# One ScalarE pass for the first layer's activation, and seven half-block products for its group 3

## The chip, the cores and the metric

The kernel runs on one core of one Trainium2 chip. TensorE (PE) multiplies matrices into PSUM, VectorE (DVE) and ScalarE (ACT) read PSUM and SBUF, GpSimd (POOL) works on SBUF alone, and SyncE (SP) issues most of the transfers. The metric is device time in microseconds (us) of one launch. Before the change the median of three runs is 619.27 us (618.97 to 619.82).

## The reference

Three stages follow each other: a windowed attention, then two feed-forward layers over its output (1536 tokens of 512 values).

```python
# attention, 2 x 8 heads, 768 tokens, head_dim 64: near scores in a window, block scores against a max per 32 keys
scores = concat(where(mask, q @ k.T * scale, -1e9), q @ kmax.T * scale + log(32))
x = softmax(scores) @ concat(v, vmean)              # -> (1536, 512)
# layer one, w_in 512 x 2048, w_out 2048 x 512
h = x @ w_in
g = h * (1.0 / (1.0 + exp(-1.702 * h)))
x = g @ w_out
# layer two, w_gate and w_val 512 x 1536, w_out2 1536 x 512
out = (1 / (1 + exp(-(x @ w_gate))) * (x @ w_val)) @ w_out2
```

## The kernel before, in words

The layers' weights are split in groups of 256 hidden columns (two blocks of 128, called f = 0 and 1): eight groups in layer one, six in layer two. The tokens are three blocks of 512 (blk 0, 1, 2). Every float32 matrix is kept as a high part and a low part (`xH`, `xL`; `w..H`, `w..L`; `gh`, `gl`), and one product of 128x128 by 512 tokens is three matmuls (low by high, high by low, high by high).

**First half of a group.** `first` (L496) computes h of one token block by `project` (L477): 12 matmuls for each f. For layer one, ACT then takes a Sigmoid of 1.702 h out of PSUM into a tile `sg` (L501), DVE multiplies h by it (`gate_by`, L485), ACT rounds the result to `gh` (L493) and POOL writes the rest, `gl` (L494). With `batch=True`, used beside the attention, the matmuls of both f come first, then both sigmoids, then both multiplications. `second` (L523) multiplies `gh`, `gl` by the output weights: 24 matmuls a block into four PSUM tiles, each then added to `acc` by DVE (L557).

**Seven products instead of eight.** For groups from `PAIRED` on, `pair` (L381) computes blk 0 and 1 together. Seen as a 2 by 2 matrix product (two halves of the input dimension LO and HI, two token blocks, two f), it takes seven half-size products of 6 matmuls rather than eight. For that it needs sums of inputs, `input_sums` (L229: eight DVE operations of 1024 elements a partition, L234, four ACT casts, four POOL subtractions), sums of the group's weights (`load`, L148 to L167: four small DVE subtractions, one ACT cast, one DVE subtraction), and it takes copies of three partial results out of PSUM on ACT (L407, L431) and two additions on DVE (L410). blk 2 goes through `single` (L448). `input_sums` is a generator; `run` steps it once for each step of the main work, from the place where `folding` is set (L919); it stops before its last steps until group `PAIRED - 1` is done with block 1, since it overwrites `xH[1]`, `xL[1]`.

**What sets the order.** The code issues work in the order that its generators yield; a scheduler then orders each engine's instructions, so an edit can move others. Beside the attention a `filler` (L825) runs groups 0 and 1 for blk 0 and 1; after it come groups 2 and 3 and the pairs. The last steps of layer one make sums of its output (`token_sums`, L274) for layer two, which pairs in the same way.

Of the kernel before, what the change touches and what calls it, by code (L numbers as in the profile page):

```python
# [9 lines left out]
F32 = mybir.dt.float32  # L10
# [3 lines left out]
AF = mybir.ActivationFunctionType  # L14
# [3 lines left out]
P = 128  # L18
# [11 lines left out]
def attention_moe_moe2_kernel(ctx: ExitStack, tc: tile.TileContext, ins: dict, out: bass.AP):  # L30
    nc = tc.nc
# [17 lines left out]
    TB = 512  # L49
# [3 lines left out]
    scale = 1.0 / float(D) ** 0.5  # L53
# [33 lines left out]
    sg_slots, gh_slots, gl_slots = (Slots(t) for t in ("sg", "gh", "gl"))  # L87
# [108 lines left out]

    mats = {1: [w_in, w_out], 2: [w_gate, w_val, w_out2]}
    pieces, weights, raws = [], {}, []
    PAIRED = 4
    wanted = [(1, g, i) for g in range(n1) for i in range(2)] + [(2, 0, i) for i in range(3)]  # L200
    for g in range(1, n2):
        wanted += [(2, h, i) for h, i in ((g, 0), (g - 1, 2), (g, 1)) if (h, i) != (0, 2)]
# [178 lines left out]
    def pair(layer, g):  # L381

        def sums_of(n, i):
            return tuple(x[:, n] for x in weights[layer, g, i, "s"])

        def a(i, r, c):
            return tuple(block(x, r, c) for x in weights[layer, g, i])

        b11, b21, b22 = ((xH[n][:, h], xL[n][:, h]) for n, h in ((0, LO), (0, HI), (1, HI)))
        left = {
            "1": lambda i: a(i, 0, 0), "2": lambda i: a(i, 0, 1), "3": lambda i: sums_of(3, i),
            "4": lambda i: a(i, 1, 1), "5": lambda i: sums_of(0, i), "6": lambda i: sums_of(1, i),
            "7": lambda i: sums_of(2, i),
        }
        right = {"1": b11, "2": b21, "3": b22, "4": tsum["4"], "5": tsum["1"], "6": tsum["2"], "7": tsum["3"]}
        bank = {"1": "x", "2": "x", "5": "v", "3": "v", "6": "y", "7": "y", "4": "y"}
        ps, held, sg = {}, {}, {}

        def new(b, i):
            ps[b, i] = ps_f.tile([P, TB], F32, name=f"ps_{b}")
            return ps[b, i]

        def keep(n, i, p):
            held[n, i] = sg_slots.tile([P, TB], F32, "sg")
            nc.scalar.copy(held[n, i], p)  # L407

        def total(n, i, p):
            nc.vector.tensor_tensor(out=held[n, i], in0=p, in1=held[n, i], op=ALU.add)  # L410
            return held[n, i]

        def out(i, to, x, own=None):
            if layer == 1:
                gate = sg_slots.tile([P, TB], F32, "sg")
                nc.scalar.activation(gate, x, AF.Sigmoid, scale=1.702)
                gate_by((1, g, *to), x, gate)
                return
            if i:
                gate_by((2, g, *to), x, sg.pop(to))  # L420
                return
            sg[to] = own if own is not None else sg_slots.tile([P, TB], F32, "sg")
            nc.scalar.activation(sg[to], x, AF.Sigmoid)

        for n in ("1526374", "1256734")[layer - 1]:
            for i in range(layer):
                b = bank[n]
                p = new(b, i) if n in "15" else ps[b, i]
                product(p, left[n](i), right[n], n in "15")
                if n == "1":  # L430
                    nc.scalar.copy(new("y", i), p)  # L431
                elif n == "2":
                    out(i, (0, 0), p)
                elif n == "5":
                    keep("5", i, p)
                elif n == "6":
                    keep("6", i, p)
                elif n == "7":
                    t = total("5", i, p)
                    out(i, (1, 1), t, t)  # L440
                elif n == "3":
                    t = total("6", i, p)
                    out(i, (1, 0), t, t)
                else:
                    out(i, (0, 1), p)
                yield

    def single(layer, g):  # L448

        for f in range(GF):  # L450
            sg = None
            for i in range(layer):
                wh, wl = weights[layer, g, i]
                ps = ps_f.tile([P, TB], F32, name="ps_h" if i == 0 else "ps_v")
                for j in range(2):
                    half = (LO, HI)[j]
                    product(ps, (block(wh, f, j), block(wl, f, j)), (xH[2][:, half], xL[2][:, half]), j == 0)
                    if j == 0:
                        yield
                if i == 0:  # L460
                    sg = sg_slots.tile([P, TB], F32, "sg")
                    nc.scalar.activation(sg, ps, AF.Sigmoid, scale=1.702 if layer == 1 else 1.0)
                if i == layer - 1:
                    gate_by((layer, g, 2, f), ps, sg)
                yield

    acc, gt = {}, {}
# [15 lines left out]
    def gate_by(to, val, sg):  # L483

        nc.vector.tensor_tensor(out=sg, in0=val, in1=sg, op=ALU.mult)  # L485
        split(to, sg)

    def split(to, sg):
        name = "_".join(map(str, to))
        gh = gh_slots.tile([P, TB], F32R, f"gh{name}")  # L490
        gl = gl_slots.tile([P, TB], F32R, f"gl{name}")
        gt[to] = gh, gl
        nc.scalar.copy(gh, sg)  # L493
        nc.gpsimd.tensor_tensor(out=gl, in0=sg, in1=gh, op=ALU.subtract)  # L494

    def first(layer, g, blk, batch=False):  # L496
        w = weights[layer, g, 0]

        def sigmoid(layer, ps):
            sg = sg_slots.tile([P, TB], F32, "sg")  # L500
            nc.scalar.activation(sg, ps, AF.Sigmoid, scale=1.702 if layer == 1 else 1.0)  # L501
            return sg

        def gated(f, ps, sg):
            gate_by((layer, g, blk, f), ps, sg)

        if batch:
            held = []
            for f in range(GF):
                held.append(project(w[0], w[1], f, blk, "ps_h"))  # L510
                yield
            held = [(ps, sigmoid(layer, ps)) for ps in held]
            yield
            for f, (ps, sg) in enumerate(held):
                gated(f, ps, sg)
            yield
            return
        for f in range(GF):
            ps = project(w[0], w[1], f, blk, "ps_h")
            gated(f, ps, sigmoid(layer, ps))  # L520
            yield

    def second(layer, g, blk, last, lag=False):  # L523
# [355 lines left out]
    with tc.manual_schedule(engines={mybir.EngineType.SP}):  # L879
# [29 lines left out]
        for step in steps:  # L909
            need((*step[:2], 0))  # L910
            run(first(*step))
            if step[2] == 2:
                drop(*step[:2], 0)
            if prev:
                need((*prev[:2], 1))
                run(second(*prev, False))
                if prev[2] == 2:
                    drop(*prev[:2], 1)
            if step == (1, 2, 0):  # L919
                folding = itertools.islice(sums_1, 8)  # L920
            elif step == (1, PAIRED - 1, 1):
                for _ in folding:
                    pass
                folding = sums_1
            prev = step
# [101 lines left out]
```

## Time and profile before

| what | value |
|---|---|
| median of three runs | 619.27 us |
| the profiled execution's own time | 619.4 us |
| its span, first to last instruction | 617.6 us |
| mean granted TensorE clock | 0.997 |
| busy: PE, DVE, ACT, POOL | 603.2, 465.9, 307.3, 212.7 us |

The span is what the profile can be read on; 1.8 us lie around it. A busy share says how much of the span an engine was at work, not whether it was waited for. A matmul's own duration (0.39 us) is a latency, as matmuls overlap: the pace is the distance between two starts. What counts is where PE stood idle, and what it did between.

### The profile page before, as it was taken

What the parts mean: (1) busy time and instruction counts of PE and PEld (TensorE: products, weight loads), DVE (VectorE), ACT (ScalarE), POOL (GpSimd) and SP (SyncE); (2) the same over time, 40 slices, a digit from 0 to 9 for tenths busy, and PEclk for the clock granted to TensorE, in tenths of its full rate; (3) what the DMA queues carried; (4) which work ended last, traced back from release to release, by engine and by line L of the source; (5) the groups of instructions that cost most, each with busy time, mean ns of one, the idle gap of its engine ahead of it and who ended that gap; (6) DMA issues with size and microseconds to landing.
All of it is one profiled execution on the core that took longest, in us unless ns stands there. A gap on an engine that the chain in (4) does not pass through costs nothing.

```text
span 617.6 us, 8819 instructions
## 1 busy us (share of the span) xinstructions
PE 603.2 (98%) x3354; PEld 501.7 (81%) x3354; DVE 465.9 (75%) x684; ACT 307.3 (50%) x614; POOL 212.7 (34%) x168
## 2 busy tenths in 40 slices
PE   7798999999999999999999999999999999999997
PEld 4676777788878888888888898888898898898896
DVE  6699665389998778797769889577969768877434
ACT  4688657556443353435445566635335335444230
POOL 6797585323363423233231232022122021131030
PEclk9899999999999999999999999999999999999999
DMA  9998753034221104040102013321312222100014
GB/s 314 347 313 286 232 137 70 1 121 153 68 69 68 53 17 137 1 137 10 60 0 69 1 40 101 132 69 33 105 69 69 68 69 70 68 1 1 0 49 156
DMA packets 25161, 58.10 MB, mean 94 GB/s; under 512 B 1568, under 2 KB 1824, under 8 KB 25120
## 3 DMA queue, kind: packets, MB, share of 16 engines
q1 hardware_dynamic: 24400, 56.24, 28.0%
q10 hardware_dynamic: 720, 1.31, 0.6%
q8 instruction: 26, 0.43, 0.3%
q14 instruction: 15, 0.12, 0.1%
HBM read 53.08 MB, written 3.15 MB: 91 GB/s over the span
## 4 chain that ended last, share of the span: by engine, by line
PE 81%; DVE 8%; ACT 3%; issue 3%; DMA 2%; POOL 2%; SPq 0%; ACTq 0%; POOLq 0%; DVEq 0%
PE ps_o L474 32%; PE ps_y L178 15%; PE ps_x L178 10%; PE ps_v L178 10%; PE ps_h L474 5%; PE ps_h L178 4%; PE ps_s L692 2%; ACT e L705 1%; PE ps_x L744 1%; DMA raw<-in_moe_w_out 1%; POOL gl L494 1%; DMA vt<-in_vt 1%; PE ps_p L725 1%; DVE da L137 1%; DVE w_0L L142 1%
## 5 line engine op out<-in xcount | busy, mean ns | idle before, releaser
L494 POOL TENSOR_TENSOR gl<-sg,gh 128x512 fp32r<-128x512 f32 x84 | 125.9, 1505 | 362.1 <-ACT gh L493 256.2
L557 DVE TENSOR_TENSOR acc<-ps_o,acc 128x512 f32<-128x512 f32 x143 | 95.9, 683 | 46.7 <-PE ps_o L474 46.6
L474 PE MATMUL ps_o<-gl,w_1H 128*128 128x512 f32 x192 | 75.5, 394 | 0.5 <-POOL gl L494 0.5
L493 ACT CAST gh<-sg 128x512 fp32r<-128x512 f32 x84 | 51.5, 620 | 48.0 <-DVE sg L485 38.6
L474 PE MATMUL ps_o<-gh,w_1H 128*128 128x512 f32 x192 | 74.6, 390 | 0.0
L474 PE MATMUL ps_o<-gh,w_1L 128*128 128x512 f32 x192 | 72.1, 396 | 1.9 <-ACT gh L493 1.7
L474 PE MATMUL ps_o<-w_2L,gh 128*128 128x512 f32 (+1 forms) x146 | 56.6, 388 | 0.0
L474 PE MATMUL ps_o<-w_2H,gh 128*128 128x512 f32 (+1 forms) x146 | 56.2, 386 | 0.0
L474 PE MATMUL ps_o<-w_2H,gl 128*128 128x512 f32 (+1 forms) x146 | 56.2, 389 | 0.1
L137 DVE SCALAR_TENSOR_TENSOR da<-da,db 128x1024 uint32<-128x1024 uint32 x34 | 46.1, 1357 | 5.7 <-ACT da L131 5.1
L131 ACT ACTIVATE da<-da 128x1024 f32<-128x1024 f32 x34 | 36.1, 1061 | 24.7 <-DVE da L123 22.9
L474 PEld LDWEIGHTS ps_o<-gh,w_1L 128*128 128x128 f32 x192 | 35.9, 188 | 9.9 <-ACT gh L493 2.3
L474 PEld LDWEIGHTS ps_o<-gl,w_1H 128*128 128x128 f32 x192 | 36.0, 188 | 8.5 <-POOL gl L494 1.5
L474 PEld LDWEIGHTS ps_o<-gh,w_1H 128*128 128x128 f32 x192 | 36.1, 188 | 7.3
L705 ACT ACTIVATE e<-ps_s,nm 128x128 f32<-128x128 f32 x96 | 34.2, 377 | 9.6 <-DVE nm L697 7.1
L681 POOL TENSOR_SCALAR kx<-k 128x384 f32<-128x384 f32 x24 | 33.3, 1389 | 14.6 <-PE ps_s L692 7.5
L474 PE MATMUL ps_h<-xH,w_0L 128*128 128x512 f32 x96 | 37.7, 401 | 0.0
L474 PE MATMUL ps_h<-xL,w_0H 128*128 128x512 f32 x96 | 37.6, 392 | 0.0
L474 PE MATMUL ps_h<-xH,w_0H 128*128 128x512 f32 x96 | 37.5, 390 | 0.0
L485 DVE TENSOR_TENSOR sg<-ps_h,sg 128x512 f32<-128x512 f32 x32 | 21.7, 682 | 14.1 <-ACT sg L501 11.9
L474 PEld LDWEIGHTS ps_o<-w_2H,gh 128*128 128x128 f32 x146 | 27.4, 188 | 5.8
L474 PEld LDWEIGHTS ps_o<-w_2L,gh 128*128 128x128 f32 x146 | 27.5, 188 | 4.9
(242 smaller groups left out, 1504.5 us busy)
## 6 DMA issues: line engine op xcount, KB each, us to landing
raw<-in_moe_w_out SPq DMA_DIRECT2D x13, 1024.0 KB, 4.9
raw<-in_moe_w_in SPq DMA_DIRECT2D x8, 1024.0 KB, 7.0
raw<-in_moe_w_gate SPq DMA_DIRECT2D x6, 1024.0 KB, 5.1
raw<-in_moe_w_val SPq DMA_DIRECT2D x6, 1024.0 KB, 5.1
q<-in_q SPq DMA_DIRECT2D x20, 256.0 KB, 8.5
vwin<-in_v SPq DMA_DIRECT2D x6, 768.0 KB, 8.6
k<-in_k SPq DMA_DIRECT2D x8, 400.0 KB, 7.2
out<-acc SPq DMA_DIRECT2D x11, 256.0 KB, 2.0
```

The source lines that it names most:

```text
L131: nc.scalar.activation(af, af, AF.Prelu, scale=REBIAS, alpha=-2.0 ** 32)
L137: nc.vector.scalar_tensor_tensor(out=a, in0=a, scalar=3, in1=b, op0=ALU.logical_shift_left, op1=ALU.bitwise_or)
L142: nc.vector.tensor_tensor(out=lo.rearrange(flat), in0=af, in1=hi.rearrange(flat), op=ALU.subtract)
L178: nc.tensor.matmul(ps, lhsT=a[x][:, kk, :], rhs=b[y][:, kk, :], start=start and i == 0, stop=i == n - 1, skip_group_check=True,)
L474: nc.tensor.matmul(ps, lhsT=a, rhs=b, start=i == 0, stop=i == n - 1)
L485: nc.vector.tensor_tensor(out=sg, in0=val, in1=sg, op=ALU.mult)
L493: nc.scalar.copy(gh, sg)
L494: nc.gpsimd.tensor_tensor(out=gl, in0=sg, in1=gh, op=ALU.subtract)
L557: nc.vector.tensor_tensor(out=a[:, m, :], in0=ps, in1=a[:, m, :], op=ALU.add)
L681: nc.gpsimd.tensor_scalar(out=to, in0=x, scalar1=scale, scalar2=None, op0=ALU.mult)
L692: nc.tensor.matmul(ps[:, j, :], lhsT=t[:, j, :], rhs=kt[:, j, :], start=False, stop=j == G - 1)
L705: nc.scalar.activation(e[:, j, :], s[:, j, :], AF.Exp, bias=nm[:, j:j + 1], accum_out=sm[:, j:j + 1])
```

## The change

Layer one's gate is written by one ACT pass of `Gelu_apprx_sigmoid` from PSUM (or from the summed tile) into `sg`, through a new helper `gated`; Sigmoid and DVE's multiplication go. Layer two keeps its Sigmoid and multiplication. `PAIRED` goes from 4 to 3, so group 3 is computed by `pair` and `single`, and `load` makes weight sums for it. `folding` starts at step (1, 1, 2) rather than (1, 2, 0); the operations in `input_sums` stay on the engines that they were on.

```diff
-    PAIRED = 4
+    PAIRED = 3
...
         def out(i, to, x, own=None):
             if layer == 1:
-                gate = sg_slots.tile([P, TB], F32, "sg")
-                nc.scalar.activation(gate, x, AF.Sigmoid, scale=1.702)
-                gate_by((1, g, *to), x, gate)
+                gated((1, g, *to), x)
                 return
...
-                if i == 0:
-                    sg = sg_slots.tile([P, TB], F32, "sg")
-                    nc.scalar.activation(sg, ps, AF.Sigmoid, scale=1.702 if layer == 1 else 1.0)
-                if i == layer - 1:
-                    gate_by((layer, g, 2, f), ps, sg)
+                gated((layer, g, 2, f), ps)
                 yield
...
+    def gated(to, x):
+
+        sg = sg_slots.tile([P, TB], F32, "sg")
+        nc.scalar.activation(sg, x, AF.Gelu_apprx_sigmoid)
+        split(to, sg)
...
         if batch:
             held = []
             for f in range(GF):
                 held.append(project(w[0], w[1], f, blk, "ps_h"))
                 yield
-            held = [(ps, sigmoid(layer, ps)) for ps in held]
-            yield
-            for f, (ps, sg) in enumerate(held):
-                gated(f, ps, sg)
+            for f, ps in enumerate(held):
+                gated((layer, g, blk, f), ps)
+            yield
             yield
             return
         for f in range(GF):
             ps = project(w[0], w[1], f, blk, "ps_h")
-            gated(f, ps, sigmoid(layer, ps))
+            gated((layer, g, blk, f), ps)
             yield
...
-            if step == (1, 2, 0):
+            if step == (1, 1, 2):
                 folding = itertools.islice(sums_1, 8)
```

Three places show what the scheduler makes of it. The first is ACT at the first filler block, after the projections of group 0, blk 0. In the names, `gh_0_0_0` is group 0, blk 0, f 0; `e,sm` are the attention's exponentials; the number at a name's end is only a buffer's. Before:

```order
L501 ACT_TABLE_LOAD
L501 ACTIVATE sg<-ps_h 128x512 x2
L140 CAST w_1_1H<-da 128x1024
L762 CAST xH_765<-ps_x 128x256
L493 CAST gh_0_0_0_793<-sg 128x512
L705 ACT_TABLE_LOAD
L705 ACTIVATE e,sm<-ps_s,nm 128x128 x4
L493 CAST gh_0_0_1_798<-sg 128x512
```

And the same place now:

```order
L485 ACT_TABLE_LOAD
L485 ACTIVATE sg<-ps_h 128x512 x2
L493 CAST gh_0_0_0_790<-sg 128x512
L493 CAST gh_0_0_1_796<-sg 128x512
L140 CAST w_1_1H<-da 128x1024
L753 CAST xH_765<-ps_x 128x256
L696 ACT_TABLE_LOAD
L696 ACTIVATE e,sm<-ps_s,nm 128x128 x4
```

Both `gh` casts now stand directly behind the activations and ahead of the weight cast, the table load and the four exponentials.

The second place is PE at the same point: `ps_p` are the attention's transposes, `ps_x` its last product, `ps_o` the filler's second half. Before:

```order
L725 MATMUL ps_p<-ident,e 128x128 x4
L744 MATMUL ps_x<-pt,vwin 64x64 x8
L474 MATMUL ps_o<-gh_0_0_0_793,w_0_1L 128x512
L692 MATMUL ps_s<-kx_805,q_584 128x128 x4
L474 MATMUL ps_o<-gh_0_0_0_793,w_0_1L 128x512
L725 MATMUL ps_p<-ident,e 128x128 x4
L474 MATMUL ps_o<-gl_0_0_0_794,w_0_1H 128x512
```

And now:

```order
L716 MATMUL ps_p<-ident,e 128x128 x4
L468 MATMUL ps_o<-gh_0_0_0_790,w_0_1L 128x512 x2
L735 MATMUL ps_x<-pt,vwin 64x64 x8
L716 MATMUL ps_p<-ident,e 128x128 x4
L468 MATMUL ps_o<-gl_0_0_0_791,w_0_1H 128x512
L468 MATMUL ps_o<-gh_0_0_0_790,w_0_1H 128x512
L468 MATMUL ps_o<-gh_0_0_1_796,w_0_1L 128x512
```

The first two `ps_o` matmuls moved ahead of `ps_x`, and the product `ps_s` of a later unit moved behind. Counted over PE's whole order, the places where an attention matmul and a matmul on the split values of the layers stand next to each other are 57 before and 47 now.

The third place is POOL behind the attention: `t1L`, `t3L`, `t2L` and `xL` are its four subtractions for the input sums, the `gl` tiles are named as the `gh` ones. Before:

```order
L494 TENSOR_TENSOR gl_2_1_0_1896<-sg,gh_2_1_0_1895 128x512
L258 TENSOR_TENSOR t1L<-f_1899,t1H 128x1024
L494 TENSOR_TENSOR gl_2_1_1_1924<-sg,gh_2_1_1_1923 128x512
L256 TENSOR_TENSOR t3L<-f_1901,t3H 128x1024
L270 TENSOR_TENSOR t2L<-f_1900,t2H 128x1024
L494 TENSOR_TENSOR gl_2_2_0_1995<-sg,gh_2_2_0_1994 128x512
L494 TENSOR_TENSOR gl_2_2_1_2022<-sg,gh_2_2_1_2021 128x512
```

And now:

```order
L494 TENSOR_TENSOR gl_1_2_0_1713<-sg,gh_1_2_0_1712 128x512
L258 TENSOR_TENSOR t1L<-f_1802,t1H 128x1024
L494 TENSOR_TENSOR gl_1_2_1_1734<-sg,gh_1_2_1_1733 128x512
L256 TENSOR_TENSOR t3L<-f_1804,t3H 128x1024
L270 TENSOR_TENSOR t2L<-f_1803,t2H 128x1024
L494 TENSOR_TENSOR gl_2_0_0_1798<-sg,gh_2_0_0_1797 128x512
L494 TENSOR_TENSOR gl_2_0_1_1826<-sg,gh_2_0_1_1825 128x512
L494 TENSOR_TENSOR gl_2_1_0_1896<-sg,gh_2_1_0_1895 128x512
L268 TENSOR_TENSOR xL_766<-f_1804,xH_765 128x1024
L494 TENSOR_TENSOR gl_2_1_1_1919<-sg,gh_2_1_1_1918 128x512
```

The first three subtractions stand three `gl` tiles earlier, and `xL`, which stood after group 3's last `gl`, now stands before group 2's `gl_2_1_1`. On DVE the first six input sums and all of group 3's weight sums lie within the 17 instructions behind the last `acc` addition of the filler. ACT's order holds one table load more, ahead of layer two's first Sigmoid; SP's order is the same as before, row for row. PE's order holds 2052 matmuls of 512 columns on split values instead of 2058.

## Rows read from the trace of the kernel before

**Rows 1.** The page, busy us (share of the span) and instructions of each engine

```profile
PE 603.2 (98%) x3354; PEld 501.7 (81%) x3354; DVE 465.9 (75%) x684; ACT 307.3 (50%) x614; POOL 212.7 (34%) x168
```

**Rows 2.** Stretch, its us, busy us (x): PE PEld DVE ACT POOL, PEclk, DMA, GB/s

```profile
40.00:60.00 20.00, 18.21 (x166) 14.28 (x162) 19.07 (x34) 18.07 (x56) 16.58 (x15) 1.00 0.99 323
60.00:80.00 20.00, 19.27 (x136) 15.28 (x136) 13.79 (x26) 13.17 (x35) 13.53 (x14) 1.00 0.68 214
80.00:100.00 20.00, 19.94 (x166) 15.78 (x165) 11.36 (x27) 11.17 (x46) 13.57 (x16) 1.00 0.51 125
...
180.00:200.00 20.00, 19.54 (x86) 15.52 (x85) 18.23 (x24) 7.50 (x11) 7.68 (x6) 1.00 0.26 93
200.00:220.00 20.00, 20.00 (x90) 16.57 (x89) 14.69 (x21) 7.17 (x11) 7.29 (x4) 1.00 0.17 54
...
600.00:620.00 20.00, 14.39 (x75) 12.06 (x74) 8.43 (x14) 1.42 (x3) 2.58 (x2) 0.97 0.35 131
```

**Rows 3.** The chain that ended last: start us, us, what

```profile
188.34 5.44 PE ps_h L474 x24
```

**Rows 4.** PE in order of time: start, us, what, [idle before <- releaser]

```profile
54.83 0.69 PE L744 MATMUL ps_x<-pt,vwin 128*64 128x64 f32 x16
57.23 0.50 PE L474 MATMUL ps_o<-gh,w_1L 128*128 128x512 f32 x1 [1.71 <-ACT gh L493]
...
63.99 0.69 PE L744 MATMUL ps_x<-pt,vwin 128*64 128x64 f32 x16 [0.62 <-DVE pt L730]
```

**Rows 5.** ACT in order of time at the first filler block

```profile
54.37 1.08 ACT L501 ACTIVATE sg<-ps_h 128x512 f32<-128x512 f32 x2
55.34 1.05 ACT L140 CAST w_1H<-da 128x1024 fp32r<-128x1024 f32 x1
...
56.54 0.64 ACT L493 CAST gh<-sg 128x512 fp32r<-128x512 f32 x1
```

**Rows 6.** PE in order of time, between attention and filler

```profile
81.97 0.50 PE L474 MATMUL ps_o<-gl,w_1H 128*128 128x512 f32 x1
82.31 0.39 PE L474 MATMUL ps_o<-gh,w_1H 128*128 128x512 f32 x1
...
86.04 0.40 PE L474 MATMUL ps_o<-gh,w_1H 128*128 128x512 f32 x1
86.37 0.69 PE L744 MATMUL ps_x<-pt,vwin 128*64 128x64 f32 x16
```

**Rows 7.** PE in order of time, from group 3's first projection on

```profile
176.25 0.39 PE L474 MATMUL ps_h<-xH,w_0L 128*128 128x512 f32 x1
...
181.69 0.39 PE L474 MATMUL ps_o<-gh,w_1L 128*128 128x512 f32 x1
...
183.50 0.50 PE L474 MATMUL ps_o<-gl,w_1H 128*128 128x512 f32 x1 [0.46 <-POOL gl L494]
...
184.99 0.40 PE L474 MATMUL ps_o<-gl,w_1H 128*128 128x512 f32 x1
```

**Rows 8.** Groups of instructions: busy us, mean ns of one, idle before

```profile
L485 DVE TENSOR_TENSOR sg<-ps_h,sg 128x512 f32<-128x512 f32 x32 | 21.7, 682 | 14.1 <-ACT sg L501 11.9 <-POOL gl L494 2.1
L501 ACT ACTIVATE sg<-ps_h 128x512 f32<-128x512 f32 x24 | 13.9, 592 | 8.6 <-PE ps_h L474 8.6
L501 ACT ACT_TABLE_LOAD x4 | 5.1, 1283 | 2.9 <-PE ps_h L474 2.9
```

**Rows 9.** DVE in order of time: two operations of 1024 elements at layer one's end

```profile
340.86 2.31 DVE L284 TENSOR_TENSOR acc<-acc,acc 128x1024 f32<-128x1024 f32 x1
343.09 1.21 DVE L291 TENSOR_TENSOR t2L<-acc,t2H 128x1024 fp32r<-128x1024 f32 x1
```

**Rows 10.** POOL, ACT and PE in order of time, layer one's end

```profile
340.00 2.09 POOL L494 TENSOR_TENSOR gl<-sg,gh 128x512 fp32r<-128x512 f32 x1 [5.94 <-ACT gh L493]
...
343.20 1.05 ACT L289 CAST yH<-acc 128x1024 fp32r<-128x1024 f32 x1 [2.80 <-DVE acc L284]
...
346.39 0.39 PE L178 MATMUL ps_y<-t2L,s_0H 128*128 128x512 f32 x1
```

More of the change, by code (lines that the diff above doesn't have):

```diff
@@ L497, in first @@
         w = weights[layer, g, 0]
[L499 to L505, printed above, removed]
         if batch:
```

## The prediction, made before the changed kernel was run

> **What bounds the kernel now.** I read the page's busy shares first: PE is at work for 603.2 of 617.6 us, while DVE has 75% and ACT 50% [rows 1]. So the question is not which engine is free, but where PE still stands idle and how much it has to do. The stretches of 20 us answer the first part [rows 2]. Between 40 and 60 us PE is not full: the DMA engines are at a share of 0.99, and DVE and ACT at 19 and 18 of 20. From 60 us to 600 us PE loses 0.73, 0.06 and 0.46 us in three stretches; the 24 others read 19.99 or 20.00, as the one at 200 us. The last stretch ends 2.4 us early with the span and holds 3.2 us of output tail, which this change does not touch. The chain of waits says the same: from some 80 us on it is nearly nothing but PE, in pieces such as 24 matmuls in 5.44 us, so 226.7 ns each [rows 3]. Behind 60 us, then, a microsecond saved on DVE or ACT is worth nothing unless PE waits for it; a matmul less is worth 226.7 ns.
>
> The waits of PE that this change can reach are three. At 55.5 us PE has done `ps_x` and waits 1.71 us for the first `gh`; at 63.4 us it waits 0.62 us for `pt`, the copy of a transposed attention tile that DVE makes [rows 4]; at 183.0 us it waits 0.46 us for a `gl` of POOL [rows 7].
>
> **The change part by part.**
>
> *Group 3 by seven products.* Blocks 0 and 1 took 2 x 24 matmuls and take 7 x 6 = 42; block 2 keeps its 24. Six matmuls go: 6 x 226.7 ns = 1.36 us, all on the path. What it adds lies on DVE (four weight sums and two additions of at most 512 elements, one subtraction of 1024: no more than 6 x 0.68 + 1.21 = 5.3 us [rows 8, 9]) and on ACT (a cast of 1024 at 1.05 us [rows 5], three copies of 512 like the sigmoid's 0.59 [rows 8]: 2.8 us), and needs cover. In place of group 3's first projection, at 176.25 us before [rows 7], the first product starts; the input sums' first use stands 25 matmuls later, 5.7 us. Six input sums, group 3's weight sums and the weight steps among them are 17 DVE instructions behind the filler. If that ends near 131 us, some 200 matmuls (200 x 0.2267 = 45 us) ahead of group 3, and each took the longest that an operation of 1024 elements took, 2.31 us [rows 9], they would be done after 39 us, at 170 us. They are at hand at least 10 us early, more likely 30. I cost it at nothing. `xL` on POOL now stands before `gl_2_1_1`, whose use is PE's next-but-one block, some 10 us after its matmuls end; a 1024-element subtraction there fits.
>
> *The input sums begun earlier.* The stall at 183 us came from them: POOL's `t2L` stood right before `gl_2_2_0` and `gl_2_2_1`. Now `t1L` to `t2L` stand among `gl_1_2_1` and `gl_2_0_0`, each with a whole first half of a block (24 matmuls, 5.44 us) before its use. The stall goes, and it is worth more than its 0.46 us: from 181.69 to 184.99 there are ten steps, 3.30 us where the pace gives 2.27, so 1.03 us [rows 7]. I take 1.0.
>
> *One ACT pass.* 48 DVE multiplications go (32 of them the group at 682 ns [rows 8], the 16 others alike): 32.8 us of DVE, worth nothing directly behind 80 us. ACT's pass has no row. Bounds: the Sigmoid on the same tile, 592 ns, from below; twice that from above. I take 592, as it is the same instruction on the same tile. At twice, 48 x 0.59 = 28 us go to an engine that is idle for half of the span; it would cost only beside the attention, in eight passes, at most 4.7 us if nothing hid them.
>
> The page "ScalarE: Activation LUTs" of the Trainium skill, section "What ACT_TABLE_LOAD costs", says that a pass takes the same time for every function, 186 ns + 0.833 ns an element; for 512 elements I estimate 613 ns from it. That would leave the sum as it is; no run here shows the new function yet.
>
> What the pass is worth beside the attention is read from the first filler block. Before, ACT ends the two sigmoids at 55.45 us, then does a weight cast and an `xH` cast while DVE multiplies, and ends the first `gh` at 57.18 [rows 5]; PE goes on at 57.23. Now `gh` follows at once: 55.45 + 0.6 = 56.05 us. But PE's order has turned too: the first two `ps_o` stand before `ps_x`, so PE waits from 54.83, where `ps_x` would have begun, to 56.05, that is 1.22 us instead of 1.71: 0.5 us won. The wait of 0.62 us for `pt` goes as well: DVE loses two multiplications ahead of that copy, and by the new order PE has twelve `ps_o` matmuls to do between two `ps_x`. Together 1.1 us.
>
> The cost of this turn is on ACT: the second `gh` cast now stands before the four exponentials, which start 0.6 us later. Behind them wait the row sums, DVE's reciprocal, POOL's scaling and the next transposes. PE has the 24 matmuls of `ps_o` for cover, 5.4 us.
>
> *Fewer switches on PE.* Going from a filler matmul to an attention one costs 86.37 - 86.04 - 0.23 = 0.10 us more than the pace, coming back 82.31 - 81.97 - 0.23 = 0.11 [rows 6]. There are ten such places fewer, 1.0 us at most, nothing if these are places where PE had to wait anyway. I take 0.8, as PE is full from 64 us on.
>
> *The table load.* One more, 1.28 us [rows 8], ahead of layer two's first Sigmoid. ACT has an idle time of 2.80 us there [rows 10], waiting for a sum by DVE; it is hidden. If that idle time were gone it would cost its 1.28.
>
> *Sum.* 1.36 + 1.0 + 1.1 + 0.8 = 4.3 us. New waits of PE that I cannot place, since most of the order has moved: between none and 2.3 us (one like the longest here, 1.71, and one like the 0.62); I take 0.8, near the 0.62. So 3.5 us, and the profiled execution's 619.4 us becomes 615.9. It stands 0.1 above the median of the runs, 619.27, so I predict 615.8 us.
>
> **The rivals.** *The attention sets its own pace.* Up to some 120 us PE mixes both, and if the chain of exponentials, scaling and transposes, now 0.6 us later, ends last, then what is won at 57 us comes back as waits further on. For it: ACT and DVE are at 18 and 19 of 20 until 60 us. Against it: behind 64 us PE is full and 24 matmuls lie between. It would leave 1.36 + 1.0 = 2.4 us: 616.9, with some waits more up to 617.9.
>
> *The six matmuls come back too.* Group 3's pair adds 2.8 us of ACT and puts more on DVE between 131 and 150 us, where it must also drain `ps_o`; a wait of 1.7 us in layer one would eat the saving. For it: four PSUM tiles are all that `second` has. Against it: groups 4 to 7 run in just this way with PE at 20.00 of 20. Then 618.3 to 619.4: no change that can be told.
>
> *Slower: layer one's end.* There DVE makes the sums for layer two in a row; up to `t2L` it does eight operations of 1024 elements. `t2L` was ready at 344.3 us and PE took it at 346.39 [rows 9, 10]: 2.1 us in hand. One of the eight took 2.31 us instead of 1.21, beside a POOL subtraction that ended at 342.09. If the new order lays POOL's work beside all of them, 8 x 1.1 - 2.1 = 6.7 us are lost: 615.8 + 6.7 = 622.5. It passes the bound to slower when six of the eight are hit. The page "SBUF — State Buffer" of the Trainium skill, section "Who interferes with whom", gives the reason: a DVE operation with two SBUF inputs and a GpSimd operation that reads SBUF exclude each other for a whole instruction. By that rule the trace agrees: 342.09 + 1.1 = 343.2, where the operation of 340.86 ended. Against it: POOL has few instructions there.
>
> *It doesn't do what it says.* If ACT needed a table load at each pass in turn with its weight steps, 1.28 us at a time would show; the order holds only one more, so I give this nothing of its own.
>
> **How the numbers follow.** The forecast 0.57 (615.8, own range 614.7 to 616.9), the attention's pace 0.23 (616.9 to 617.9), the saving eaten 0.13 (618.3 to 619.4), layer one's end 0.07 (622.5). Two executions of this kernel can't be told apart below about 0.2%, 1.24 us: faster is below 618.0, slower above 620.5. Faster 0.57 + 0.22 = 0.79, the same 0.14, slower 0.07. The range for 8 in 10 leaves out the slowest case and most of the third: 614.4 to 618.7. Its lower end is the full 4.3 us without new waits and another half microsecond of switches.
>
> **What would show it.** PE has 3348 matmuls; no wait for `gl` near 180 us; the first `ps_o` at about 56 us; PE at 20.00 from 64 us on; the new ACT pass at 0.6 us; DVE busy some 29 us less. Wrong would be: waits of PE on ACT's `e` or `pt` between 60 and 120 us (then the attention sets the pace), waits in the stretch around group 3, or on `t2L` near 340 us.

## The result: slower by 5.7 us, and the profile after

The changed kernel takes 625.29 us (median of 4 runs, 624.82 to 625.39), the kernel before 619.55 in the same session: a ratio of 1.0100, 95% interval 1.0088 to 1.0112. Forecast were 615.8 us and a range of 614.4 to 618.7. The profiled execution has a span of 623.6 us against 617.6.

The page's busy shares of the changed kernel answer to [rows 1]:

```profile
PE 605.3 (97%) x3347; PEld 502.7 (81%) x3348; DVE 447.9 (72%) x643; ACT 311.6 (50%) x619; POOL 211.2 (34%) x168
```

Six matmuls are gone, as forecast (a record or so is missing here), yet PE is busy 2 us longer. DVE lost 48 multiplications, 32.8 us, got seven small operations for group 3 (5.3 us at most by the prediction), and is busy only 18 us less: what is left has become longer. The stretches of the changed kernel (columns as in [rows 2]) tell where PE lost time:

```profile
100.00:120.00 20.00, 19.09 (x160) 14.88 (x159) 7.63 (x20) 14.26 (x48) 9.00 (x9) 1.00 0.06 12
...
160.00:180.00 20.00, 16.65 (x60) 12.46 (x58) 19.90 (x20) 9.89 (x13) 7.74 (x5) 0.83 0.32 105
180.00:200.00 20.00, 19.79 (x86) 16.07 (x87) 16.16 (x24) 7.46 (x12) 4.12 (x3) 1.00 0.31 106
```

From 160 to 180 us PE does 60 matmuls where 90 fit, and its granted clock is 0.83. In the kernel before the same stretch was full, and DVE with it:

```profile
160.00:180.00 20.00, 20.00 (x90) 16.57 (x89) 20.00 (x20) 8.82 (x12) 12.59 (x6) 1.00 0.24 65
```

The changed kernel's PE there, in order of time, with its waits in brackets:

```profile
160.81 0.39 PE L468 MATMUL ps_h<-xH,w_0H 128*128 128x512 f32 x1
163.36 0.47 PE L468 MATMUL ps_o<-gh,w_1L 128*128 128x512 f32 x1 [2.16 <-DVE acc L548]
...
166.13 0.79 PE L468 MATMUL ps_o<-gh,w_1L 128*128 128x512 f32 x1 [1.04 <-DVE acc L548]
166.72 0.63 PE L468 MATMUL ps_o<-gl,w_1H 128*128 128x512 f32 x1
167.15 0.63 PE L468 MATMUL ps_o<-gh,w_1H 128*128 128x512 f32 x1
...
171.42 0.46 PE L468 MATMUL ps_o<-gh,w_1L 128*128 128x512 f32 x1
...
180.15 0.50 PE L468 MATMUL ps_o<-gh,w_1L 128*128 128x512 f32 x1 [0.29 <-DVE acc L548]
```

PE waits for DVE's additions `acc`, which empty the PSUM tiles `ps_o`. From 160.81 to 171.42 us there are 19 steps: at 226.7 ns [rows 3] they take 4.31 us, here 10.61, so 6.30 us are lost. Waits are 3.20 of that. The 12 steps from 166.13 to 171.42 take 5.29 us in place of 2.72: there the granted clock is 0.50, half speed or 1.2 GHz, and the matmuls follow each other in steps of 0.43 us. That costs 2.57 us. The rest, 0.53, is the restart behind the waits. The third wait adds 0.45 us (0.68 from 179.47 to 180.15, less a step). In all 6.75 us.

What DVE did before, in order of time (changed kernel; `ws` and `s_0L` belong to the weight sums, `f` to the input sums, L123 and L137 are steps that unpack the weights):

```profile
144.41 4.07 DVE L156 TENSOR_TENSOR ws<-da 128x256 f32<-128x256 f32 x2
148.41 2.61 DVE L156 TENSOR_TENSOR ws<-ws,da 128x256 f32<-128x256 f32 x1
...
153.21 0.41 DVE L156 TENSOR_TENSOR ws<-da,ws 128x256 f32<-128x256 f32 x1
...
155.36 2.59 DVE L165 TENSOR_TENSOR s_0L<-ws,s_0H 128x1024 fp32r<-128x1024 f32 x1 [1.00 <-ACT s_0H L163]
157.98 1.67 DVE L123 TENSOR_SCALAR db<-raw 128x1024 uint32<-128x1024 uint32 x1
159.76 2.13 DVE L137 SCALAR_TENSOR_TENSOR da<-da,db 128x1024 uint32<-128x1024 uint32 x1
161.92 0.69 DVE L123 TENSOR_SCALAR db<-raw 128x1024 uint32<-128x1024 uint32 x1
162.53 0.68 DVE L548 TENSOR_TENSOR acc<-ps_o,acc 128x512 f32<-128x512 f32 x1
```

And what POOL did beside it:

```profile
143.60 3.17 POOL L258 TENSOR_TENSOR t1L<-f,t1H 128x1024 fp32r<-128x1024 f32 x1 [3.15 <-PE ps_o L468]
146.71 1.49 POOL L494 TENSOR_TENSOR gl<-sg,gh 128x512 fp32r<-128x512 f32 x1
148.17 2.57 POOL L256 TENSOR_TENSOR t3L<-f,t3H 128x1024 fp32r<-128x1024 f32 x1
154.46 2.41 POOL L270 TENSOR_TENSOR t2L<-f,t2H 128x1024 fp32r<-128x1024 f32 x1 [3.72 <-ACT t2H L266]
157.50 3.31 POOL L494 TENSOR_TENSOR gl<-sg,gh 128x512 fp32r<-128x512 f32 x2 [0.63 <-ACT gh L493]
```

An operation on 256 elements takes 0.41 us at 153.21, with POOL idle, and 2.61 at 148.41, until just behind the end of `t3L` (150.74). PE started to write the four tiles at 150.15 us; their first addition came at 162.53, since DVE works in its written order. By 161.04 PE wanted the first tile back. From 130.62 us, behind the filler's last `acc`, to this addition DVE does 21 operations in 31.9 us. At the lengths that such operations have in this trace beside an idle POOL (twelve of 1.21 to 1.23 us, five of L123 at 0.68, four of `ws` at 0.41), and with the wait of 1.00 us for ACT, they would take 20.6 us, an estimate from these rows: the addition would stand near 151 us, ten before PE needs the tile.

Long operations alone cost nothing, as the kernel before shows. There the same `t1L` to `t2L` ran 22 us later, and DVE's operations beside them were as long:

```profile
165.51 3.43 POOL L258 TENSOR_TENSOR t1L<-f,t1H 128x1024 fp32r<-128x1024 f32 x1 [2.85 <-ACT t1H L254]
167.19 2.83 DVE L234 TENSOR_TENSOR f<-f,f 128x1024 f32<-128x1024 f32 x1
169.94 0.68 DVE L557 TENSOR_TENSOR acc<-ps_o,acc 128x512 f32<-128x512 f32 x1
```

But between its input sums stood additions (164.86, 166.59, 169.94 and 171.65 us), and PE was full. In the changed kernel the first six input sums and group 3's weight sums stand ahead of the first addition with none between them.

### The profile page after: what moved, and what is told of

Read it like the earlier page. It is cut to its first block, busy times and chain, and to the rows that moved or that the text cites. A ratio compares the mean times of both kernels' runs of the same rounds, so it can differ in the third digit from the quotient of the medians.

```text
span 623.6 us, 8761 instructions
## 1 busy us (share of the span) xinstructions
PE 605.3 (97%) x3347; PEld 502.7 (81%) x3348; DVE 447.9 (72%) x643; ACT 311.6 (50%) x619; POOL 211.2 (34%) x168
## 4 chain that ended last, share of the span: by engine, by line
PE 83%; DVE 9%; ACT 4%; issue 2%; DMA 1%; POOL 1%; SPq 0%; ACTq 0%; DVEq 0%; POOLq 0%
PE ps_o L468 33%; PE ps_y L178 15%; PE ps_v L178 10%; PE ps_x L178 10%; PE ps_h L178 4%; PE ps_s L683 3%; PE ps_h L468 3%; PE ps_x L735 2%; DVE f L234 2%; ACT e L696 2%; DVE ws L156 2%; PE ps_p L716 1%; DVE da L137 1%; DMA vt<-in_vt 1%; POOL gl L494 1%
## 5 line engine op out<-in xcount | busy, mean ns | idle before, releaser
L468 PE MATMUL ps_o<-gh,w_1H 128*128 128x512 f32 x192 | 75.9, 395 | 0.0
L137 DVE SCALAR_TENSOR_TENSOR da<-da,db 128x1024 uint32<-128x1024 uint32 x34 | 50.0, 1471 | 9.0 <-ACT da L131 8.4
L672 POOL TENSOR_SCALAR kx<-k 128x384 f32<-128x384 f32 x24 | 31.1, 1299 | 13.7 <-DMA k<-in_k 6.8
L683 PEld LDWEIGHTS ps_s<-kx,q 128*128 128x128 f32 x192 | 27.4, 219 | 5.5 <-POOL kx L672 2.7
L468 PEld LDWEIGHTS ps_o<-w_2H,gl 128*128 128x128 f32 x146 | 27.4, 188 | 5.2 <-DVE acc L548 0.3
L683 PE MATMUL ps_s<-kx,q 128*128 128x128 f32 x192 | 30.3, 310 | 1.2 <-POOL kx L672 1.2
L123 DVE TENSOR_SCALAR db<-raw 128x1024 uint32<-128x1024 uint32 x33 | 30.1, 911 | 1.3 <-DMA raw<-in_moe_w_out 0.8
```

Source lines behind the costliest of these rows:

```text
L123: ins = nc.vector.tensor_scalar(**x)
L137: nc.vector.scalar_tensor_tensor(out=a, in0=a, scalar=3, in1=b, op0=ALU.logical_shift_left, op1=ALU.bitwise_or)
L468: nc.tensor.matmul(ps, lhsT=a, rhs=b, start=i == 0, stop=i == n - 1)
L672: nc.gpsimd.tensor_scalar(out=to, in0=x, scalar1=scale, scalar2=None, op0=ALU.mult)
L683: nc.tensor.matmul(ps[:, j, :], lhsT=t[:, j, :], rhs=kt[:, j, :], start=False, stop=j == G - 1)
```

## The experiments

Each time is the median, and the ratio is to the kernel before in its own session. The last two columns come from the profile: the start of the attention's last group of `ps_x` matmuls, and what is left from there to the span's end.

| kernel | us | ratio to before, 95% interval | last `ps_x` | from there |
|---|---|---|---|---|
| before | 619.55 | | 123.83 | 493.8 |
| changed | 625.29 | 1.0088 to 1.0112 | 124.92 | 498.7 |
| act_alone | 620.52 | 1.0014 to 1.0032 | 123.92 | 494.4 |
| pair_alone | 627.38 | 1.0123 to 1.0151 | 122.43 | 502.9 |
| no_group3_sums | 624.51 | 1.0077 to 1.0108 | 124.84 | 496.6 |
| lows_on_dve | 621.04 | 1.0017 to 1.0041 | 125.35 | 494.3 |
| gl_dve_lows_pool | 619.61 | 0.9993 to 1.0011 | 125.07 | 493.0 |
| lows_gl_dve | 617.81 | 0.9961 to 0.9982 | 123.53 | 491.3 |
| lows_gl_dve_no_pair | 619.52 | 0.9994 to 1.0011 | 124.73 | 493.4 |
| sigmoid_lows_gl_dve | 616.68 | 0.9949 to 0.9976 | 123.27 | 491.2 |
| cast_late | 625.44 | 1.0087 to 1.0121 | 124.30 | 499.4 |
| lows_dve_cast_late | 621.12 | 1.0020 to 1.0040 | 124.61 | 494.9 |
| old_filler | 616.48 | 0.9935 to 0.9962 | 124.05 | 491.3 |
| act_old_filler | 621.99 | 1.0026 to 1.0059 | 123.67 | 496.5 |
| filler_only | 616.85 | 0.9967 to 0.9986 | 123.50 | 491.2 |
| first_block_new | 616.45 | 0.9954 to 0.9978 | 123.51 | 491.3 |

### Which part of the change costs the time

act_alone:

```diff
-    PAIRED = 3
+    PAIRED = 4
-            if step == (1, 1, 2):
+            if step == (1, 2, 0):
```

> The kernel before with the activation pass alone: groups 0 to 3 stay in whole products, and the input sums start with group 2's first block, as before. Theory (VectorE's queue: the earlier input sums and group 3's weight sums, which stand ahead of acc_2's additions on VectorE, hold the ps_o tiles at 163 us): no wait of TensorE for acc between 140 and 185 us and a granted clock of 1.0 there, PE 20.00 of 20 in 160:180; about 619 us (617.5 to 620), since the stall at 183 goes (-0.5 to -1) and the attention may end up to 0.95 us later as it does in the changed kernel. Rival 1 (the activation pass itself costs the time, by the order of the engines in the attention or by what it does to ACT): 622 to 625 us, with acc waits or a late attention. Rival 2 (the six matmuls and the pair for group 3 matter little, all is in the activation): same as the changed kernel, 625.

pair_alone is the kernel before with the opposite edit (4 to 3, and the earlier step).

> The kernel before with group 3 by seven products and the input sums begun at the same step as in the changed kernel, but the activation still a Sigmoid on ScalarE and a multiplication on VectorE (48 more VectorE instructions in layer one than the changed kernel, one per tile). Theory (VectorE's queue in 130 to 180 us is overfull): the stall at 163 us is there and is longer, since eight multiplications of 0.6 to 0.7 us stand in the same stretch: 626 to 630 us, the waits for acc or for the sg multiplication 5 us or more, and the clock at 0.5 again. Rival 1 (the activation pass costs the time): 617 to 620 us, as the six matmuls less give 1.36. Rival 2 (the order that the scheduler happened to choose, not the amount): anything, with the order of the additions deciding.

no_group3_sums leaves the four `ws` operations of group 3 out; the cast and the subtraction behind them read the unpacked weights instead, so its output is another.

> The changed kernel without the four additions that make group 3's weight sums (group 3's seven products read the split of the first weights in their place, so the values of the output differ; all casts, splits, DMAs and matmuls are kept). Theory (amount of VectorE work ahead of acc_2's additions): ws additions took 4.07 for two, 2.61 and about 2 us there, so acc_2's additions come 6 to 8 us earlier, the waits at 163, 166 and 180 us go or fall below 1 us, the clock stays 1.0, and the time falls by 4 to 6.5 us to 619 to 621. Rival (the input sums begun early are enough to fill the queue): 623 to 625, with a wait for acc of 2 us or more left. Rival 2 (activation): 625.

The pair with its earlier input sums costs 8.3 us by itself, as its theory said; the activation pass alone 1.4, with two short waits for `acc`, of 0.49 and 0.37 us, so both the theory's bound and rival 1 were missed. In pair_alone these are PE's waits for `ps_o` between 40 and 200 us (us in all, times, longest):

```profile
PE ps_o L474 <- DVE acc L557: 3.7, 2, 2.5
PE ps_o L474 <- POOL gl L494: 2.0, 1, 2.0
PE ps_o L474 <- ACT gh L493: 2.0, 2, 1.6
```

All but ACT's 1.6 lie between 169 and 187 us. The changed kernel, with both parts, lies between the two. But without group 3's sums a wait of 2.69 us for `acc` stays, and the time is only 0.8 us lower than the changed kernel's, as the rival said: the `ws` work that I had named first is not the cause. By this run alone the six input sums could still be too much work for DVE; the next three speak against that.

### GpSimd beside VectorE

lows_on_dve makes this edit for `l1` to `l4` (one of four shown; `tt` is a subtraction on VectorE that keeps its written place):

```diff
-        nc.gpsimd.tensor_tensor(out=l3, in0=f3, in1=h3, op=ALU.subtract)
+        tt(out=l3, in0=f3, in1=h3, op=ALU.subtract)
```

> The changed kernel with the four subtractions of the input sums' low parts (t1L, t3L, t2L, xL; 2.4 to 3.2 us each on GpSimd) on VectorE, where one of them costs 1.2 to 1.3 us undisturbed. Theory (amount on VectorE's queue): the queue gets 4 instructions longer by 5 us and the stall grows: 627 to 630. Rival (VectorE's instructions are long because they run beside GpSimd's; the ws additions of 0.41 and 0.74 us alone took 2.6 and 4.07 there): the 8 us by which its instructions in 140 to 160 us are stretched go, against 5 us added, so acc_2's additions come 2 to 4 us earlier and the time falls to 621 to 624.

lows_gl_dve does so for `gl` too; gl_dve_lows_pool has this second edit alone:

```diff
-        nc.gpsimd.tensor_tensor(out=gl, in0=sg, in1=gh, op=ALU.subtract)
+        eng = nc.vector if to[0] == 1 and acc_b is not None else nc.gpsimd
+        eng.tensor_tensor(out=gl, in0=sg, in1=gh, op=ALU.subtract)
```

> The changed kernel with the four low parts of the input sums and also every gl of layer one after the attention on VectorE, so that GpSimd runs nothing there while VectorE works: 4 instructions of 1.2 us and 44 of about 0.7 us more on VectorE, some 36 us in all. Theory (VectorE's instructions are stretched by GpSimd's that run beside them): no two-input instruction of VectorE between 130 and 180 us is over its undisturbed length (1.2 us for 1024, 0.41 for 256), except where both wait for something; acc_2's first addition comes no later than in the version with the low parts alone on VectorE (157.5 us), the waits for acc sum to under 2 us, the clock is 1.0: 618.5 to 621. Rival (amount of work on VectorE decides): the waits for acc, or new ones for gl on VectorE, are 4 us or more: 624 to 630.

> The changed kernel with only the gl of layer one after the attention on VectorE; the four low parts stay on GpSimd. It completes the square: both on GpSimd 625.3, low parts on VectorE 621.0, both on VectorE 617.8. If each instruction of GpSimd costs VectorE what it overlaps, the gl account for about as much as between the last two: 621 to 623, with long two-input instructions of VectorE only beside t1L, t3L, t2L and xL. Rival (the two do not add, the queue's order decides): 617.5 to 619 or over 624.

More work on DVE made it faster: by 4.2 us with the low parts there, 5.7 with `gl`, 7.5 with both. The first came out as its rival said, lows_gl_dve below its theory's range, and gl_dve_lows_pool between its two ranges. (The two edits do not add: either one alone takes away most of one stall.) In lows_on_dve the same operations, with two more ahead of `acc` and one of L123 moved behind it:

```profile
144.85 1.85 DVE L156 TENSOR_TENSOR ws<-da 128x256 f32<-128x256 f32 x2
146.63 0.41 DVE L156 TENSOR_TENSOR ws<-ws,da 128x256 f32<-128x256 f32 x1
...
149.57 1.21 DVE L234 TENSOR_TENSOR t1L<-f,t1H 128x1024 fp32r<-128x1024 f32 x1
150.71 1.22 DVE L234 TENSOR_TENSOR t3L<-f,t3H 128x1024 fp32r<-128x1024 f32 x1
...
157.51 0.68 DVE L548 TENSOR_TENSOR acc<-ps_o,acc 128x512 f32<-128x512 f32 x1
```

The first `acc` comes 5.0 us earlier, although two operations were put ahead of it: with the order kept, less of POOL beside DVE is enough. In lows_gl_dve nothing is stretched, the first `acc` stands at 150.62 us, and PE is full while DVE is busy all the time:

```profile
140.05 0.75 DVE L156 TENSOR_TENSOR ws<-da 128x256 f32<-128x256 f32 x2
140.72 0.42 DVE L156 TENSOR_TENSOR ws<-ws,da 128x256 f32<-128x256 f32 x1
...
150.62 0.68 DVE L549 TENSOR_TENSOR acc<-ps_o,acc 128x512 f32<-128x512 f32 x1
```

```profile
160.00:180.00 20.00, 20.00 (x90) 16.58 (x89) 20.00 (x28) 10.02 (x13) 0.00 (x0) 1.00 0.16 53
```

DVE's order is another here too, though: only two of the input sums stand ahead of this first `acc`, where the changed kernel has six, and so it is in gl_dve_lows_pool. What the new order alone is worth, with POOL's work as it was, no run shows.

In gl_dve_lows_pool one wait of 1.5 us for `acc` is left, at 181.86 us, and ahead of it DVE is stretched just where POOL's `t1L` and `t3L` (160.26 to 168.69 us) have moved:

```profile
164.15 2.30 DVE L495 TENSOR_TENSOR gl<-sg,gh 128x512 fp32r<-128x512 f32 x1
166.37 2.60 DVE L156 TENSOR_TENSOR ws<-da,ws 128x256 f32<-128x256 f32 x1
```

### What the two parts are worth without that

lows_gl_dve_no_pair is lows_gl_dve with the edit of act_alone. sigmoid_lows_gl_dve is pair_alone with both moves to VectorE.

> The same with group 3 back in whole products (six matmuls more, no weight sums for it) and the input sums begun at group 2's first block, as in the kernel before. It tells what the pair for group 3 is worth when no engine is held up. Theory (six matmuls at 226.7 ns): 1.0 to 1.8 us slower than lows_gl_dve. Rival (its sums on VectorE take it back through waits of TensorE even without GpSimd beside them): the same within 0.5 us, or faster than lows_gl_dve.

> pair_alone (Sigmoid and multiplication, group 3 by seven products) with the four low parts and every gl after the attention on VectorE. Theory (what stretched VectorE's instructions was GpSimd, and TensorE waits only when the additions come late): pair_alone's 627.4 falls by 5 us or more, to 618 to 622, although VectorE gets some 40 instructions more. Rival (VectorE has room for gl only because the one pass took 48 multiplications from it): the waits for acc and for the multiplication or gl stay at 3 us or more and the time at 625 to 632.

The pair is worth 1.7 us by the medians (2.1 behind the attention), a little over its six matmuls' 1.36. The one pass is worth nothing behind the attention: with Sigmoid and multiplication the time behind the attention is 491.2 us against 491.3, with some 26 us more of DVE's work (474.4 us busy against 448.5) all hidden. sigmoid_lows_gl_dve is 8.6 us under the changed kernel, more than its theory expected, and with a ratio of 0.9963 faster than the kernel before.

### The attention

In the changed kernel ACT does both casts and the table load ahead of the next exponentials, near 100 us:

```profile
100.45 0.64 ACT L493 CAST gh<-sg 128x512 fp32r<-128x512 f32 x1
101.11 1.28 ACT L696 ACT_TABLE_LOAD   x1
102.40 0.37 ACT L696 ACTIVATE e<-ps_s,nm 128x128 f32<-128x128 f32 x1
```

and PE waits until these exponentials have read their PSUM tile `ps_s`, which it wants to write again:

```profile
103.96 0.38 PE L681 MATMUL ps_s<-mask,pick 128*128 128x512 bf16 x1 [0.89 <-ACT e L696]
```

cast_late writes the second cast a step later and fixes its place in ACT's written order; lows_dve_cast_late does so in lows_on_dve (main lines of the edit):

```diff
-                gated((layer, g, blk, f), ps)
-            yield
-            yield
...
+                nc.scalar.activation(sg, ps, AF.Gelu_apprx_sigmoid)
+                done.append(sg)
+            split((layer, g, blk, 0), done[0])
+            yield
+            yield
+            split((layer, g, blk, 1), done[1], True)
```

> The changed kernel with one edit in the attention: in a filler block the cast of the second gate (gh, second half of the pair) is written one step later, so that ScalarE does the next unit's exponentials first, as it did before the change. Theory of the attention's share: in the changed kernel both casts (0.62 and 0.64 us) precede the table load, the exponentials start at 102.40 us instead of 101.31 and TensorE waits 0.89 us at 103.96 for e; with the edit that wait falls to about 0.2 and the rest of the program is 0.5 to 1.0 us earlier: 624.3 to 624.8. Rival: the later cast makes the later matmuls of `second` wait for gh or gl, and nothing is won: 625 to 626. In both the stall for acc at 163 us stays, 3 to 4 us.

> Both repairs: the four low parts on VectorE and the second cast one step later in the attention. If the two costs add (stall for acc: 4.2 us by the run with the low parts on VectorE; late exponentials: 0.5 to 1.0 us): 620.0 to 620.5, 0.5 to 1.0 under that run. Rival (the attention's end is set elsewhere and the wait only moves): 621.0 as with the low parts alone.

In both the theory missed and the rival came true: nothing was won. In cast_late the wait at 104 us went, and two others came at 104.3 and 109.1, 0.16 and 0.60 us (the second for `pt`). Its later stall is there, as expected, but earlier: 2.4 us for ACT's `acc` copies and 1.3 for DVE's, and 17.56 us of PE in 140 to 160 us.

old_filler puts the filler's old form into lows_gl_dve, act_old_filler into act_alone (main lines of the edit):

```diff
-                gated((layer, g, blk, f), ps)
-            yield
...
+                nc.scalar.activation(sg, ps, AF.Sigmoid, scale=1.702)
+                done.append((ps, sg))
+            yield
+            for f, (ps, sg) in enumerate(done):
+                gate_by((layer, g, blk, f), ps, sg)
```

> lows_gl_dve with the filler blocks of the attention as in the kernel before (Sigmoid on ScalarE, then the multiplication on VectorE, then the cast); the one pass stays in layer one after the attention. Theory (in the attention the one pass costs time, because its casts come ahead of the next exponentials; last ps_x of the attention at 123.8 us and 122.4 with the old filler, at 123.5 to 125.4 with the new one): 0.6 to 1.4 us faster than lows_gl_dve, 616.4 to 617.2; TensorE's wait of 0.87 us for e near 103 us goes, and the wait of 0.6 us for pt at 64 us comes back. Rival (the attention ends as its loads and units let it; the differences between profiles are scatter of the start): 617.5 to 618.1, the same.

> act_alone (the kernel before with the activation pass, 1.4 us slower than before) with the filler blocks of the attention as in the kernel before, so that the one pass is in layer one after the attention only. Theory (the one pass costs about a microsecond in the attention and nothing behind it): 618.5 to 619.6, the same as before; the last ps_x of the attention at 123 to 124 us and no wait of 0.9 us for e near 104. Rival (the loss of act_alone lies behind the attention, in its two waits for acc near 183 us): 620.2 to 620.8 as act_alone.

The first came out as expected, 616.48 us, the fastest but for first_block_new, which is not told apart from it; the second missed theory and rival: 1.5 us slower than act_alone. Its attention does not end later; its loss lies behind, in three waits (0.78 us for `gl`, 1.47 and 0.35 for `acc`, where act_alone has 0.49 and 0.37). DVE is stretched beside POOL there too (the two `ws` ahead of the longest wait's `acc` took 2.83 us), but no run shows that this is the whole difference. So this run says nothing on the filler.

filler_only has the one pass in the filler of sigmoid_lows_gl_dve and nowhere else, first_block_new in the first block of old_filler.

> sigmoid_lows_gl_dve (616.7) with the one activation pass in the filler blocks of the attention alone; behind the attention Sigmoid and multiplication stay, and nothing of TensorE waits there. Theory (all filler blocks in one pass cost time, because the casts come ahead of the exponentials): 617.3 to 618.2, 0.6 to 1.5 us slower, with the wait of 0.9 us for e near 103 us. Rival (the prediction's term: the filler wins 1.1 us by the earlier gh and the wait for pt that goes): 615.6. Third (no difference beyond scatter): 616.4 to 617.0.

> old_filler (616.5) with the one pass in the first filler block only (the one near 55 us), the other three as before. Prediction's term for that block alone (0.5 us by gh earlier, 0.6 by the wait for pt that goes): 615.4 to 616.0. Theory that casts ahead of exponentials cost time in every block: 616.7 to 617.2, with a wait of 1.0 to 1.2 us for e near 61 us. Third: 616.5, the loss sits in the third block, at 103 us, alone.

By the medians the one pass in all four blocks costs 0.2 us here (1.3 between lows_gl_dve and old_filler), in the first block nothing; by the ratios 0.8, 1.4 and 1.1 us. The intervals overlap in all three. So filler_only fits its third case, no difference beyond scatter; first_block_new's time fits its third one too, though no run shows that the loss sits in the block at 103 us alone. All profiles together: the last `ps_x` starts at 123.45 us on average in the five kernels with the old filler (122.43 to 124.05), at 124.48 in the eight with the one pass in its plain form and order (123.50 to 125.35): 1.0 us later with a standard error of 0.4. So no gain is there, and a loss of up to about a microsecond is likely; its size stays open.

## Why the prediction was wrong, step by step

*The step that failed* is the one on group 3: "They are at hand at least 10 us early, more likely 30. I cost it at nothing." The sums were indeed in time (`xL` ends at 173.84 us, PE takes the first sum at 190.39). I asked when the 17 instructions would be done and not what stood behind them on the same engine: the additions `acc`, which must come within some 9.5 us, as `second` has four PSUM tiles: a block of 48 matmuls, 10.9 us, less the six that fill the first tile. "Each took the longest, 2.31 us" was the right order of size (31.9 us for 21 operations came), and 17 such in a row, 39 us, was the warning: more than three blocks of PE pass in that. The price is 6.75 us, more than the whole loss of 5.7. Three runs show this. In lows_on_dve DVE's order is nearly the same and its list longer, but less is stretched, and the wait of 2.16 us goes. In lows_gl_dve both the stretching and the row of sums are gone, and with them the whole stall. no_group3_sums shows that the added `ws` work alone was not it.

*The rule I used elsewhere.* The rival "layer one's end" named this very mechanism, DVE stretched beside POOL, but at 340 us; that its 6.7 us are near the 6.75 is chance. There it did not happen: `t2L` ends at 350.3 us and PE takes it at 353.82, 3.5 us in hand. (Its sum has a slip: with six of the eight hit it gives 615.8 + 6 x 1.1 - 2.1 = 620.3, still under the 620.5.) In 140 to 160 us POOL is busy 12.50 us where it was 5.04 before, since `t1L` to `t2L` and the `gl` now meet there; I had moved these instructions on POOL's queue and judged them only by POOL's own due times. The page "SBUF — State Buffer" of the Trainium skill, section "Who interferes with whom", limits the exclusion to DVE operations with two SBUF inputs or in a two-port mode; the trace agrees: `acc`, which reads PSUM and SBUF, is never stretched (all 143 took between 0.65 and 0.69 us), while `ws` went from 0.41 to 2.61 us, `s_0L` from 1.21 to 2.59 and L123 from 0.68 to 1.78.

*"The six matmuls come back too"* was the right place (waits in layer one, four PSUM tiles) with a price of 1.7 us; the slow clock, 2.57 us, and the second and third wait were not in it.

*Six matmuls, 1.36 us, and the stall at 183 us, 1.0 us:* right, 2.36 us together. In lows_gl_dve, where nothing else interferes, the time behind the attention is 2.5 us shorter than before (491.3 against 493.8). In the changed kernel they are there too, as PE is full from 200 us on, under the 6.75; but a late `gl` came back, which POOL ended at 186.80 us, and the matmuls at 186.85 and 187.19 us lost 0.34 us by it.

*First filler block, 1.1 us, and fewer switches, 0.8 us:* not won, taken together; no run shows the switches by themselves. `gh` came as forecast; the changed kernel's PE:

```profile
56.23 0.73 PE L468 MATMUL ps_o<-gh,w_1L 128*128 128x512 f32 x2 [1.12 <-ACT gh L493]
...
60.87 0.38 PE L681 MATMUL ps_s<-mask,pick 128*128 128x512 bf16 x1 [1.21 <-ACT e L696]
```

The wait of 1.71 us became 1.12 (forecast 1.22) and that for `pt` went [rows 4], but behind the exponentials, which start at 59.31 us instead of 58.49 behind the second cast, PE waits 1.21 us at 60.87, and 0.89 at 103.96. From 50 to 126 us PE's waits sum to 3.2 us instead of 2.3. Of the 24 matmuls that I took for cover only eight stood ahead of that wait. first_block_new shows the exchange in this block alone: against old_filler the wait for `gh` is 1.11 us instead of 1.49 and that of 0.61 for `pt` is gone, but one of 1.29 us for `e` is new. That is the rival "the attention sets its own pace", which I had at 0.23.

*The ACT pass:* 592 ns forecast, 594 measured from PSUM (627 where its input is a sum in SBUF); the page "ScalarE: Activation LUTs" of the Trainium skill, section "What ACT_TABLE_LOAD costs", gave an estimate of 613, and the trace agrees to some 3%. The group of the changed kernel:

```profile
L485 ACT ACTIVATE sg<-ps_h 128x512 f32<-128x512 f32 x28 | 16.1, 594 | 7.4 <-PE ps_h L468 5.8 <-PE ps_h L178 1.6
```

The table load for layer two, at 347.35 us, is hidden, as forecast. "DVE busy some 29 us less" was wrong by 11 us, which the stretching ate.

*The sum of the loss:* +6.75 (stall) + 1.1 (attention's end, 124.92 against 123.83) - 1.36 - 1.0 = 5.5 us of the 6.0 between the spans. The late `gl` at 186.85 us is 0.34 of the 0.5 that is left; the rest I did not place.

## What to carry to other kernels

When work is moved onto an in-order engine, look first at what is queued behind it there, how long its reader can do without it (here the four PSUM tiles, one block of PE), and which instructions of the neighbouring engine now lie beside it. A length read where the neighbour was idle is a lower bound: price the operations at their stretched length. Keep the operations that empty PSUM among the others, as the kernel before did, where the same lengths cost nothing. And where DVE and POOL overlap, try moving POOL's short work onto DVE. It may be faster although DVE's list gets longer.

## What the hardware showed that I had not expected

An operation of 0.41 us took 2.61 beside a POOL operation of 2.57, so it is held for all of it, and short operations pay most for their length. POOL pays as well: `t1L` took 5.63 us in gl_dve_lows_pool, while DVE worked beside it, and 3.17 in the changed kernel; there `gl` took between 1.49 and 2.31 us from 132 to 148 us, and 1.29 at 121.36, with DVE idle for most of that time.

The clock cost 2.57 us beside 3.49 of waits. In the changed kernel PE did six matmuls behind the wait of 2.16 us, in steps of 0.23 us at a granted clock of 1.00 (163.36 to 164.59). From 164.59 to 166.13 it reads 0.54, so it had fallen when the second wait, 1.04 us, was just beginning, and it stayed at 0.50 until 171.42. One wait was enough elsewhere. In no_group3_sums, behind 2.69 us:

```profile
163.82 0.77 PE L480 MATMUL ps_o<-gh,w_1L 128*128 128x512 f32 x1 [2.69 <-DVE acc L560]
...
166.09 0.63 PE L480 MATMUL ps_o<-gh,w_1H 128*128 128x512 f32 x1
```

Six steps take 2.70 us there (clock 0.50) in place of 1.36. In cast_late the clock was 0.50 from 158.76 to 162.10 us, behind one wait of 2.44 us, and in pair_alone it is under 1.00 in two stretches on end, behind waits of 2.00 and 2.52 us:

```profile
160.00:180.00 20.00, 17.65 (x70) 13.79 (x69) 19.90 (x21) 8.98 (x13) 13.07 (x6) 0.91 0.07 16
180.00:200.00 20.00, 16.30 (x60) 12.46 (x59) 15.85 (x20) 6.31 (x9) 5.74 (x3) 0.83 0.26 90
```

It stayed at 1.00 behind the waits of 1.28 and 0.62 us in lows_on_dve, 1.49 in gl_dve_lows_pool and 1.47 in act_old_filler. So a wait can cost PE more than its own length, here up to 2.57 us more.
